# Moving a weight load to another DMA queue, moving two loads down a hand-written order, interleaving a rounding chain and closing a joint: an attention and MLP-mixer kernel

## The chip, the cores and the metric

The kernel runs on one core of one Trainium2 chip, as one launch. The metric is the device time in microseconds. The kernel before was run three times beside its profile: 807.25 us is the median, 807.18 the lowest and 807.42 the highest.

## The reference

There are 8 batches, 8 heads, 576 tokens and 64 elements to a head. First comes linear attention with a root-mean-square norm for each head; its output is laid out as 576 tokens by 512 features. On this a mixer works: a token mixing with a residual, then a channel mixing with a residual.

```python
kv  = einsum('bhsd,bhse->bhde', k, v)
out = einsum('bhsd,bhde->bhse', q, kv)
x   = out / sqrt(mean(out*out, -1) + 1e-6) * g_norm   # then (B, S, 512)
xt  = x.transpose(0, 2, 1)
u   = x + (maximum(xt @ w_tok1, 0) @ w_tok2).transpose(0, 2, 1)
y   = u + maximum(u @ w_ch1, 0) @ w_ch2
```

`w_tok1` is 576x256, `w_tok2` 256x576, `w_ch1` 512x1536 and `w_ch2` 1536x512. The weights reach the kernel as 64-bit floats, and the kernel makes 32-bit floats of them itself.

## The kernel before, in words

**Two halves.** Until about 200 us the kernel does attention and token mixing, two batches (a pair) at a time, four pairs. From there it does the channel mixing, in nine groups of 512 token rows; between the halves `u` lies in DRAM (`u_dram`).

**First half.** The order of the work is written out by hand, as strings of step names that `play` calls one after the other: `start`, `middle`, twice `steady`, and `last`. Each string runs the attention of one pair beside the token mixing of the pair before it. A name is one step: `kv10` multiplies k by v for half 0 of batch 1 of the pair, `e10` copies the product out of PSUM, `a2` multiplies q by it for a piece of tokens, `g`, `q`, `t` are the gain, the square and the sum over 64 elements of a piece, `m`, `r`, `i` make the inverse norm of a group of pieces, `s` and `p` scale with it on ScalarE and on GpSimd. `h` is the first token product (`hr` its rest, with the ReLU), `z` seeds a PSUM bank with the residual and `u` is the second token product, with its store to `u_dram`. The order in a string is the order on every engine and on every DMA queue; semaphores make one engine wait for another.

**Loads.** `l00` to `l11` load k and v of half a batch for the next pair. There are four buffers `k_in` and four `v_in`, so that `l00` can start once `kv00` of the present pair has been read. A load is four DMAs, 1.18 MB together. `lq0` and `lq1` load q. All of these, and the stores, are issued by SP's queue, in the order of the strings (`dma`, L114); only the very first v goes by ScalarE's queue.

**Weights.** A weight is fetched as raw 32-bit words (`raw`, four buffers, tag `raw`) and turned in eight steps, `block` (L202) and `decode` (L149): `fetch`, then `scale` on ScalarE (L163), then on VectorE `clamp` (L166), `shift` (L170), `sign` (L174), `power` (L183), `lower` (L187) and `both` (L118). The last step that reads `raw` is `lower`. Each step but the first two works on the result of the one before it; `part` has one buffer. The token weights are five blocks (`w00` to `w47` in the strings), the channel weights fourteen: eight of `w_ch1` (768 elements to a partition, one DMA of 786 KB) and six of `w_ch2` (1024 elements, two DMAs of 524 KB). The first four fetches of the channel weights are named in the strings, `f0` to `f3`; everything else of them is a stream (`stream`, L1048) of which a number in a string takes that many steps. In the stream `scale` of the next block goes beside `lower`, and the fetch of the block four further beside `both`.

**Second half.** The channel mixing multiplies with seven products in place of eight, twice nested. The first group does it once only (`channel1_once`, `channel2_once`), the other eight groups do both levels. A product is some matmuls into a PSUM bank; the sums are VectorE's. `channel2_once` has seven steps, `first, sixth, second, seventh, fifth, fourth, third`, with four PSUM banks from pool `m` (6 banks). `weave` (L1039) spreads VectorE work between the steps. After it all groups are one list of numbered places (`put`, `products`, `beside`); at a place first the product runs and then what was put beside it. In `outer` (L763) the first product of a group goes to a bank `a`, `read_first` copies it to a bank `ps_c` from pool `c` (2 banks), and later products are added into both.

**The joint** between the first group and the nested ones is this (L1217 to L1224): the next `xg` is fetched, and two matmuls of 128x384, whose result nobody reads, go into the two banks of pool `c`, one ahead of place 0 and one behind its product.

Of the kernel before, what the change touches and what calls it, by code (L numbers as in the profile page):

```python
# [19 lines left out]
def kernel(  # L20
# [32 lines left out]
    nc = tc.nc  # L53
# [60 lines left out]
    def dma(o, i, engine=nc.sync):  # L114
        keep(engine.dma_start(o, i))  # L115
# [83 lines left out]

        return flat if len(dst.shape) == 2 else flat.rearrange("p (a n) -> p a n", a=dst.shape[1])  # L200

    def block(n, loads, dst):  # L202

        raw = []

        def fetch():
            raw.append(stage.tile([P, n, 2], U32, name="raw", tag="raw", bufs=4))
            for o, i in loads(raw[0]):
                dma(o, i)

        def turn():
            t = raw[0]
            return t if len(dst.shape) == 2 else t.rearrange("p (a n) w -> p a n w", a=dst.shape[1])

        return (fetch,) + decode(dst, turn)
# [14 lines left out]
    def get_ch1(c, f):  # L230

        return block(2 * FQ, lambda raw: [(raw, words(moe_w_ch1)[ts(c, P), ts(f, 2 * FQ)])],
                     w_ch1[:, 2 * f + c // 2, c % 2:4:2])

    def get_ch2(f):

        a = 2 * (2 * f // NS)

        def loads(raw):
            t = raw.rearrange("p (h f n) w -> p f h n w", h=2, f=2)  # L240
            rows = words(moe_w_ch2)[ts(f, 2 * P)].rearrange("(f p) (h n) w -> f p h n w", f=2, h=2)
            return [(t[:, i], rows[i]) for i in range(2)]

        dst = w_ch2[:, a:a + 2, ds(2 * f % NS, 2)]
        return block(2 * DM, loads, dst.rearrange("p h f n -> p h (f n)"))

# [370 lines left out]
    def m_psum(shape, name):  # L619
        return late["m"].tile(shape, F32, name=name, tag="m")  # L620
# [82 lines left out]
    def channel2_once(g):  # L703

        shape = [P, 2, DH]
        x = xg[g]
        quarter = lambda i, j: x[:, 2 * i:2 * i + 2, ts(j, DH)]

        def product(n, ps, start, stop):
            for p in range(2):  # L710
                for s in range(NS):
                    matmul(ps[:, p], lhsT=late["once"][n - 1][:, s, p], rhs=w2_of(n)[:, s],
                           start=(start and p == 0 and s == 0), stop=stop,
                           skip_group_check=True)

        p1, p6, p7, p5 = (m_psum(shape, f"ps_w{n}") for n in (1, 6, 7, 5))
        t1, u2, u3 = (r_tile() for _ in range(3))

        def first():
            product(1, p1, True, False)  # L720
            copy(t1, p1)

        def sixth():
            product(6, p6, True, True)
            tensor_add(u2, p6, t1)

        def seventh():
            product(7, p7, True, False)
            tensor_add(u3, p7, u2)
            tensor_add(quarter(0, 1), quarter(0, 1), u2)  # L730
            tensor_add(quarter(1, 0), quarter(1, 0), u2)

        def fifth():
            product(5, p5, True, False)
            tensor_add(u3, p5, u3)
            tensor_add(quarter(1, 1), quarter(1, 1), u3)

        def second():
            product(2, p1, False, True)
            tensor_add(quarter(0, 0), p1, quarter(0, 0))  # L740

        def fourth():
            product(4, p7, False, True)
            tensor_add(quarter(1, 0), p7, quarter(1, 0))
            store(g, xg, 1)

        def third():
            product(3, p5, False, True)
            tensor_add(quarter(0, 1), p5, quarter(0, 1))
            store(g, xg, 0)  # L750

        return [first, sixth, second, seventh, fifth, fourth, third]
# [10 lines left out]
    def outer(place, size, mul, to, base=None, act=copy, onto=False):  # L763

        banks, t = {}, {}

        def product(n, name, start, stop):
            if start:
                banks[name] = m_psum([P, size], f"ps_{name}")
            mul(n, banks[name], start, stop)

        def temp(n, bufs):
            t[n] = late["tmp"].tile([P, FQ], F32, name=n, tag=n, bufs=bufs)[:, :size]
            t[n] = fit(t[n])
            return t[n]

        def fit(flat):
            return flat if size == P else flat.rearrange("p (w t) -> p w t", w=W)

        def read(o, i, j):

            if base:
                tensor_add(o, fit(banks["a"]), base(i, j))
            else:
                copy(o, fit(banks["a"]))

        def read_first():
            banks["c"] = late["c"].tile([P, DM], F32, name="ps_c")[:, :size]
            read(fit(banks["c"]), 0, 0)

        def write(i, j, name, n):
            tensor_add(to(i, j), fit(banks[name]), to(i, j) if onto else t[n])

        def put_on(i, j, n):
            if onto:
                tensor_add(to(i, j), to(i, j), t[n])  # L800

        def take(i, j, name, act):
            if onto:
                tensor_add(to(i, j), banks[name], to(i, j))
            else:
                act(to(i, j), fit(banks[name]))

        def at(n, name, start, stop, *steps):
            def all_of():
                product(n, name, start, stop)  # L810
                for step in steps:
                    step()

            products[place + PLACE[n]] = all_of

        at(1, "a", True, False, read_first)
        at(6, "a", False, False, lambda: read(temp("u2", 2), 0, 1))
        at(5, "b", True, False)
        at(7, "a", False, False, lambda: read(temp("u3", 1), 1, 1))
        at(2, "c", False, True, lambda: take(0, 0, "c", act))  # L820
        put(place + PLACE[7] + (1 if onto else 2), do(put_on, 1, 1, "u3"), do(write, 1, 1, "b", "u3"))
        at(4, "a", False, True, lambda: take(1, 0, "a", copy) if onto else read(to(1, 0), 1, 0))
        put(place + PLACE[4], do(put_on, 0, 1, "u2"))
        at(3, "b", False, True)
        put(place + PLACE[3] + 1, do(write, 0, 1, "b", "u2"))
# [219 lines left out]
                fill[done]()  # L1045
                done += 1

    def stream(blocks, ahead=4):  # L1048


        steps = [blocks[0][1]]
        for n, block in enumerate(blocks):
            steps += block[2:]
            for at, m, k in ((-2, n + 1, 1), (-1, n + ahead, 0)):
                if m < len(blocks):
                    steps[at] = do(lambda *fs: [f() for f in fs], steps[at], blocks[m][k])
        return iter(steps)

    def play(lines, after={}, **stages):

# [37 lines left out]
    for block in tok1[2:] + tok2:  # L1098
# [11 lines left out]
        "h010 t21 m2 r2", "a30 g30 q30 i2 p20", "a31 g31 q31 t30", "h011 t31 m3 r3 p21", "a40 i3 p30 g40 q40 p31",  # L1110
        "h012 h013 t40 m4 r4 w21 i4 s40 lq0 l10 l11"]
    middle = [
        "kv00 e00 w31 w22 w23 w24", "h10 w25 w26 w27 f1 -lq1 l00 w32 w33 w34", "kv01 e01 l01 w41 w35 w36 w37",
        "h11 f2 w42 w43 w44", "hr w45 w46 w47 f3", "a0 q00 g01 q01 g00 t00 t01", "u0 z2 1", "u1 1",
        "a1 q10 g11 q11 g10 t10 t11 m0 r0", "u2 i0 1", "kv10 e10 z4 s00", "u3 1 s01", "kv11 e11 1",
        "u4 1 z6", "a2 q20 g21 q21 g20 s10", "u5 t20 t21 2", "a4 q40 g41 q41 g40 lq0 l10 l11", "u6 t40 t41 2",
        "a3 q30 g31 q31 g30 lq1 s11", "u7 t30 t31 m2 r2 1 i2 p20 p21 s30", "u8 1 s31"]

    def steady(n0, n1):
        return [  # L1120
            "kv00 l00 e00 1 -s40", "h00 3", "kv01 l01 e01 1", "h01 3", f"a0 q00 g01 q01 g00 {n0}",
            "h10 1 t00 t01 2", "h11 4", "hr 2 z2", "a1 q10 g11 q11 g10 1", "kv10 l10 e10 t10 t11 m0 r0 1",
            "u0 i0 1", "kv11 l11 e11", "u1 1 s00", "u2 z4 1", "a2 q20 g21 q21 g20", "u3 s01 t20 t21",
            "u4 z6 1", "a4 q40 g41 q41 g40 lq0", "u5 s10 t40 t41 1", "a3 q30 g31 q31 g30 lq1",
            "u6 s11 t30 t31 m2 r2 1 i2 p20 p21 s30", f"u7 1 s31 {n1}", "u8 2"]

    attentions = [attention(0, ((0,), (1,), (2,), (3,), (4,)))]
# [3 lines left out]
    mixings.append(token_mixing(B // 2 - 1, range(2, 9), (0, 1)))  # L1131
    more = {f"w{n}{k}": f for n, b in enumerate(tok1 + tok2) for k, f in enumerate(b)}
    more |= {f"f{n}": b[0] for n, b in enumerate(channel)}
    rounding = stream(channel)

    def keep_warm(n):

# [75 lines left out]
             lambda: [f() for f in outer_u(1)], lambda: [f() for f in inner_u(1, 0, 7)]]  # L1213
    extra += [lambda: None] * (len(channel2_once_steps := channel2_once(0)) - len(extra))
    body = [step for pair in zip(channel2_once_steps, extra) for step in pair]
    weave(body, lasts + [f for fs, _ in inner2 for f in fs] + [f for _, f in inner1])
    fetch_x(1, 0)  # L1217
    fetch_x(1, 1)


    for place in range(2):
        t = late["c"].tile([P, DM], F32, name="ps_c")
        step = do(matmul, t[:, :FQ], lhsT=w_ch1[:, 0, 0, :P], rhs=w_ch1[:, 0, 0], start=True, stop=True)
        put(place, step) if place else step()  # L1224
    for n, (_, f) in enumerate(inner2):
        put(8 + n, f)
    for g in range(1, NG):
# [42 lines left out]
```

## Time and profile before

| what | value |
|---|---|
| median of three runs | 807.25 us |
| the profiled execution | 807.63 us, of which the span from first to last instruction is 805.8 us |
| busy in the span | TensorE 788.6 us (98%), VectorE 683.3 (85%), ScalarE 302.2 (38%), GpSimd 79.6 (10%) |
| granted TensorE clock | 0.999 |
| DMA | 175.51 MB, 218 GB/s over the span; 276 GB/s from 0 to 205 us |
| GpSimd | 75 instructions, none of them a DMA |

How to read it: TensorE has matmuls in flight nearly all the time, so the span can only get shorter where TensorE idles or does work that isn't needed. Where it idles is read from the timeline of TensorE, in which a bracket gives the idle time and what ended it. "SPq" is SP's queue, that is the time in which it issues a DMA; "PEld" is TensorE's load of weights. The DMA row of the page gives, for each fortieth of the span, how busy the 16 DMA engines were.

### The profile page before, as it was taken

The page shows a single profiled execution, that of the slowest core. Times are in us where ns is not written, and L with a number is a line of the kernel's source. Part 1 is how long each engine was busy: PE and PEld are TensorE (multiplying, and loading weights), DVE is VectorE, ACT ScalarE, POOL GpSimd, SP SyncE. Part 2 cuts the span into 40 slices and gives each one's busy share as a digit, 9 for nine tenths or more (in the row PEclk, how much of TensorE's full clock was granted, in tenths as well). Part 3 has the DMA queues.
Part 4 walks back from the last instruction along what each step waited for, and adds up shares of the span by engine and source line. Part 5 has one row for each costly group of instructions (what it writes and reads, how often), then busy time and mean ns, then how long its engine had stood idle before and what let it go on. Part 6 is the DMA issues. An engine that isn't in the chain of part 4 may idle for free.

```text
span 805.8 us, 17651 instructions
## 1 busy us (share of the span) xinstructions
PE 788.6 (98%) x7012; PEld 694.4 (86%) x7012; DVE 683.3 (85%) x1308; ACT 302.2 (38%) x838; POOL 79.6 (10%) x75
## 2 busy tenths in 40 slices
PE   6999999999999999999999999999999999999997
PEld 6645554544888899999999999999999999999997
DVE  4688989999886978978987997997898899799687
ACT  1357585664110134234234234332424423423331
POOL 1210101010000011012003003001101200300300
PEclk9999999999999999999999999999999999999999
DMA  9999998436458567468467648738836855863642
GB/s 289 320 345 351 334 354 304 158 119 208 150 175 294 194 210 239 131 221 267 149 201 240 201 153 259 234 118 262 265 119 217 262 166 181 250 201 123 218 147 83
DMA packets 97346, 175.51 MB, mean 218 GB/s; under 512 B 7024, under 2 KB 54128, under 8 KB 97264
## 3 DMA queue, kind: packets, MB, share of 16 engines
q1 hardware_dynamic: 95584, 172.65, 66.6%
q10 hardware_dynamic: 1680, 1.74, 0.7%
q8 instruction: 55, 0.90, 0.5%
q14 instruction: 27, 0.22, 0.1%
HBM read 137.79 MB, written 36.57 MB: 216 GB/s over the span
## 4 chain that ended last, share of the span: by engine, by line
PE 83%; DVE 6%; DMA 5%; ACT 3%; SPq 1%; issue 1%; ACTq 0%; DVEq 0%
PE ps_a L127 37%; PE ps_b L127 19%; PE ps_c L127 9%; PE ps_v L127 5%; PE ps_w L127 4%; PE ps_u L127 4%; DMA v_in<-in_v_dram 3%; PE ps_h L127 2%; ACT x L475 1%; SPq L115 1%; DMA raw<-in_moe_w_ch_dram 1%; DMA k_in<-in_k_dram 1%; DVE ms L442 1%; DVE part L187 1%; DVE x L421 1%; PE ps_o L127 1%
## 5 line engine op out<-in xcount | busy, mean ns | idle before, releaser
L124 ACT COPY u<-ps_a 128x128 f32<-128x128 f32 (+1 forms) x160 | 56.1, 351 | 156.6 <-PE ps_a L127 156.6
L118 POOL TENSOR_TENSOR v<-v,v 128x384 f32<-128x384 f32 (+1 forms) x48 | 61.4, 1301 | 532.8 <-ACT v L124 492.8
L127 PE MATMUL ps_b<-uT,sums 128*128 128x128 f32 x672 | 86.2, 276 | 0.0
L127 PEld LDWEIGHTS ps_b<-uT,sums 128*128 128x128 f32 x672 | 80.7, 192 | 0.2
L118 DVE TENSOR_TENSOR v<-v,v 128x768 f32<-128x768 f32 (+1 forms) x86 | 79.5, 932 | 1.1
L127 PE MATMUL ps_a<-uT,w_ch 128*128 128x128 f32 x576 | 78.9, 275 | 0.0
L124 ACT COPY ps_c<-ps_a 128x128 f32<-128x128 f32 (+1 forms) x80 | 26.9, 336 | 129.5 <-PE ps_a L127 129.5
L118 DVE TENSOR_TENSOR v<-ps_b,u 128x384 f32<-128x384 f32 x112 | 61.5, 549 | 12.3 <-PE ps_b L127 10.6
L127 PEld LDWEIGHTS ps_a<-uT,w_ch 128*128 128x128 f32 x576 | 71.4, 192 | 0.4
L127 PE MATMUL ps_u<-h,w_tok 128*128 128x512 f32 (+1 forms) x160 | 68.0, 608 | 1.6 <-ACT h L121 0.6
L127 PE MATMUL ps_h<-x,w_tok 128*128 128x512 f32 (+1 forms) x160 | 65.9, 604 | 0.0
L118 DVE TENSOR_TENSOR uT<-uT 128x512 f32<-128x512 f32 (+4 forms) x103 | 63.1, 629 | 0.8
L127 PE MATMUL ps_a<-uT,w 128*128 128x128 f32 x432 | 60.0, 275 | 0.0
L127 PEld LDWEIGHTS ps_a<-uT,w 128*128 128x128 f32 x432 | 54.0, 192 | 0.0
L127 PEld LDWEIGHTS ps_h<-x,w_tok 128*128 128x128 f32 (+1 forms) x160 | 25.9, 189 | 31.1 <-issue 28.3
L127 PEld LDWEIGHTS ps_u<-h,w_tok 128*128 128x128 f32 (+1 forms) x160 | 24.5, 178 | 31.9 <-issue 24.9
L121 ACT ACTIVATE v<-v 128x384 f32<-128x384 f32 (+1 forms) x86 | 42.5, 528 | 23.0 <-DVE v L118 22.5
L118 DVE TENSOR_TENSOR sv<-v 128x384 f32<-128x384 f32 x80 | 43.4, 551 | 8.9 <-ACT v L121 8.9
L118 DVE TENSOR_TENSOR xg<-xg,r 128x512 f32<-128x512 f32 x74 | 50.0, 686 | 0.7
L475 ACT ACTIVATE x<-x,inv 128x64 f32<-128x64 f32 x184 | 46.0, 336 | 9.6 <-DVE inv L461 9.6
L127 PE MATMUL ps_a<-sums,sv 128*128 128x128 f32 x336 | 47.1, 276 | 0.0
L127 PE MATMUL ps_a<-uT,sums 128*128 128x128 f32 x336 | 46.8, 275 | 0.0
(134 smaller groups left out, 1576.5 us busy)
## 6 DMA issues: line engine op xcount, KB each, us to landing
sums<-sums SPq DMA_DIRECT2D x112, 576.0 KB, 4.4
qT<-in_q_dram SPq DMA_DIRECT2D x8, 1152.0 KB, 9.6
xt<-u_dram SPq DMA_DIRECT2D x36, 256.0 KB, 4.0
blocks<-y SPq DMA_DIRECT2D x72, 128.0 KB, 2.7
uT<-blocks SPq DMA_DIRECT2D x36, 256.0 KB, 4.9
xg<-u_dram SPq DMA_DIRECT2D x18, 512.0 KB, 5.1
k_in<-in_k_dram SPq DMA_DIRECT2D x16, 512.0 KB, 9.2
u_dram<-x SPq DMA_DIRECT2D x16, 512.0 KB, 4.9
```

Of the source, the lines that this page charges most:

```text
L115: keep(engine.dma_start(o, i))
L118: keep(engine.tensor_tensor(out=o, in0=a, in1=b, op=op))
L121: keep(nc.scalar.activation(o, a, AF.Relu))
L124: keep(nc.scalar.copy(o, a))
L127: keep(nc.tensor.matmul(*a, **kw))
L187: keep(nc.vector.scalar_tensor_tensor(out=part[0], in0=raw()[..., 0], scalar=2.0 ** -52, in1=part[0], op0=ALU.mult, op1=ALU.mult))
L421: keep(nc.vector.tensor_mul(x, bank[c, h], g_sb.to_broadcast([P, number(c), D])))
L442: keep(nc.vector.tensor_reduce(stats_of(c)[0][:, h], sq[c, h], axis=AX.X, op=ALU.add))
L475: keep(nc.scalar.activation(x[:, k, h], x[:, k, h], AF.Copy, scale=inv[:, k, h]))
```

## The change

It has four parts.

- **Loads later.** `l00` to `l11` of `middle` and `steady` stand further down in the strings. One number of `middle` (`u8 1`) is now 2.
- **Rounding in turns.** For the six blocks of `w_ch2` the stream no longer does the six VectorE steps of a block in a row: `clamp`, `shift`, `sign` of a block alternate with `power`, `lower`, `both` of the block before. `scale` of the next block goes beside `shift`, and the fetch of the block four further beside `lower`. Blocks of `w_ch1` stay as they were.
- **Joint.** The two matmuls without a reader are gone. `channel2_once` takes two of its four banks (`p7`, `p5`) from pool `c`; its last step, `third`, runs behind the first product of place 0, and the two fetches of `xg` behind that.
- **Queue.** The fetches of the channel weights are issued by GpSimd's queue, those of the token weights by SP's as before. GpSimd keeps its scalings `p` in its own order with them.

```diff
-    def block(n, loads, dst):
+    def block(n, loads, dst, engine=nc.sync):
...
-                dma(o, i)
+                dma(o, i, engine)
...
-                     w_ch1[:, 2 * f + c // 2, c % 2:4:2])
+                     w_ch1[:, 2 * f + c // 2, c % 2:4:2], nc.gpsimd)
...
-        return block(2 * DM, loads, dst.rearrange("p h f n -> p h (f n)"))
+        return block(2 * DM, loads, dst.rearrange("p h f n -> p h (f n)"), nc.gpsimd)
...
-        p1, p6, p7, p5 = (m_psum(shape, f"ps_w{n}") for n in (1, 6, 7, 5))
+        p1, p6 = (m_psum(shape, f"ps_w{n}") for n in (1, 6))
+        p7, p5 = (late["c"].tile(shape, F32, name="ps_c", tag="c") for _ in range(2))
...
-            banks["c"] = late["c"].tile([P, DM], F32, name="ps_c")[:, :size]
+            banks["c"] = late["c"].tile([P, DM], F32, name="ps_c", tag="c")[:, :size]
...
-    def stream(blocks, ahead=4):
+    def stream(blocks, turns, ahead=4):
+        def all_of(*fs):
+            return do(lambda: [f() for f in fs])
         steps = [blocks[0][1]]
-        for n, block in enumerate(blocks):
-            steps += block[2:]
-            for at, m, k in ((-2, n + 1, 1), (-1, n + ahead, 0)):
-                if m < len(blocks):
-                    steps[at] = do(lambda *fs: [f() for f in fs], steps[at], blocks[m][k])
-        return iter(steps)
+        second = []
+        for n in range(len(blocks)):
+            _, _, *first = blocks[n]
+            if n + 1 < len(blocks):
+                k = 1 if n >= turns else 4
+                first[k] = all_of(first[k], blocks[n + 1][1])
+            if n + ahead < len(blocks):
+                k = 4 if n >= turns else 5
+                first[k] = all_of(first[k], blocks[n + ahead][0])
+            if n < turns:
+                steps += first
+            else:
+                pairs = zip(first[:3], second or [None] * 3)
+                steps += [f for pair in pairs for f in pair if f]
+                second = first[3:]
+        return iter(steps + second)
...
     middle = [
-        "kv00 e00 w31 w22 w23 w24", "h10 w25 w26 w27 f1 -lq1 l00 w32 w33 w34", "kv01 e01 l01 w41 w35 w36 w37",
-        "h11 f2 w42 w43 w44", "hr w45 w46 w47 f3", "a0 q00 g01 q01 g00 t00 t01", "u0 z2 1", "u1 1",
+        "kv00 e00 w31 w22 w23 w24", "h10 w25 w26 w27 f1 -lq1 w32 w33 w34", "kv01 e01 w41 w35 w36 w37",
+        "h11 f2 w42 w43 w44", "hr l00 w45 w46 w47 f3", "a0 q00 g01 q01 g00 t00 t01", "u0 z2 1", "u1 l01 1",
...
-        "u4 1 z6", "a2 q20 g21 q21 g20 s10", "u5 t20 t21 2", "a4 q40 g41 q41 g40 lq0 l10 l11", "u6 t40 t41 2",
-        "a3 q30 g31 q31 g30 lq1 s11", "u7 t30 t31 m2 r2 1 i2 p20 p21 s30", "u8 1 s31"]
+        "u4 1 z6", "a2 q20 g21 q21 g20 s10", "u5 t20 t21 2", "a4 q40 g41 q41 g40 lq0", "u6 t40 t41 2 l10",
+        "a3 q30 g31 q31 g30 lq1 s11", "u7 t30 t31 m2 r2 1 i2 p20 p21 s30", "u8 2 l11 s31"]
     def steady(n0, n1):
-            "kv00 l00 e00 1 -s40", "h00 3", "kv01 l01 e01 1", "h01 3", f"a0 q00 g01 q01 g00 {n0}",
-            "h10 1 t00 t01 2", "h11 4", "hr 2 z2", "a1 q10 g11 q11 g10 1", "kv10 l10 e10 t10 t11 m0 r0 1",
-            "u0 i0 1", "kv11 l11 e11", "u1 1 s00", "u2 z4 1", "a2 q20 g21 q21 g20", "u3 s01 t20 t21",
-            "u4 z6 1", "a4 q40 g41 q41 g40 lq0", "u5 s10 t40 t41 1", "a3 q30 g31 q31 g30 lq1",
+            "kv00 e00 1 -s40", "h00 3", "kv01 e01 1", "h01 3", f"a0 q00 g01 q01 g00 l00 {n0}",
+            "h10 1 t00 t01 2", "h11 l01 4", "hr 2 z2", "a1 q10 g11 q11 g10 1", "kv10 e10 t10 t11 m0 r0 1",
+            "u0 i0 1", "kv11 e11", "u1 1 s00 l10", "u2 z4 1", "a2 q20 g21 q21 g20", "u3 s01 t20 t21",
+            "u4 z6 1 l11", "a4 q40 g41 q41 g40 lq0", "u5 s10 t40 t41 1", "a3 q30 g31 q31 g30 lq1",
...
-    rounding = stream(channel)
+    rounding = stream(channel, 2 * NC)
...
     body = [step for pair in zip(channel2_once_steps, extra) for step in pair]
+    behind = body.pop(-2)
     weave(body, lasts + [f for fs, _ in inner2 for f in fs] + [f for _, f in inner1])
-    fetch_x(1, 0)
-    fetch_x(1, 1)
-    for place in range(2):
-        t = late["c"].tile([P, DM], F32, name="ps_c")
-        step = do(matmul, t[:, :FQ], lhsT=w_ch1[:, 0, 0, :P], rhs=w_ch1[:, 0, 0], start=True, stop=True)
-        put(place, step) if place else step()
+    put(0, behind, do(fetch_x, 1, 0), do(fetch_x, 1, 1))
```

## The prediction

> **What bounds the kernel now.** I read the page first, then TensorE's timeline for its gaps, then the chain of waits.
>
> ```profile
> PE   6999999999999999999999999999999999999997
> DVE  4688989999886978978987997997898899799687
> DMA  9999998436458567468467648738836855863642
> ```
>
> TensorE is full after the first fortieth. DMA is full for six to seven slices (to about 135 us), and VectorE is nearly full from slice 5 to 10. The span is 805.8 us and TensorE busy 788.6, so 17.2 us are idle: 6.7 ahead of the first matmul, about 5 in the tail (21.1 us busy from 780 to 806), the rest, some 5.5, in small gaps between 20 and 165 us. From 165 to 780 us there is none: a microsecond saved before it is a microsecond of the result.
>
> The gaps that the change can reach, from the timelines of TensorE, ScalarE and VectorE:
>
> ```profile
> 26.13 1.39 PE L127 MATMUL ps_kv<-v_in,k_in 128*64 128x64 f32 x40 [0.94 <-DMA v_in<-in_v_dram]
> ...
> 100.00 0.94 ACT L163 ACTIVATE w_ch<-raw 128x768 f32<-128x768 f32 x1 [7.70 <-DMA raw<-in_moe_w_ch_dram]
> ...
> 103.93 0.69 DVE L421 TENSOR_TENSOR x<-ps_o,g_sb 128x512 f32<-128x512 f32 x1 [1.68 <-ACT sq L425]
> ...
> 161.93 1.16 PE L127 MATMUL ps_o<-kvp,qT 64*64 64x64 f32 x64 [1.12 <-ACT sq L425]
> ```
>
> Read the bracket: the idle time, and what ended it. `kv11` of the first pair waits for its v. At 100 us ScalarE has stood 7.7 us before a `scale` whose raw weight is late; behind it stand the ReLUs of `hr` and the squares, so VectorE loses 1.68 us and TensorE 0.57. At 161.93 `a3` waits for a square, which waits for a gain (L421) that stands behind rounding in VectorE's queue.
>
> The chain of waits (start, length, what) says how the first and the second came about:
>
> ```profile
> 15.82 10.17 DMA v_in<-in_v_dram
> 26.13 1.39 PE ps_kv L127 x40
> ...
> 79.20 9.54 DMA v_in<-in_v_dram
> 88.75 2.00 SPq L115
> 90.85 9.13 DMA raw<-in_moe_w_ch_dram
> 100.95 1.95 ACT h L121 x4
> ```
>
> A load of v lands, only then does SP's queue come to the raw fetch.
>
> **The Trainium skill.** (1) "DMA: Bandwidth & Descriptors", section "Issuing engines are not separate DMA queues": DMAs of all issuers run on the same 16 engines and interleave, and "Queues, rings and completion order": an engine goes round-robin between its queue rows. The trace agrees as far as it goes: from 15 to 27 us the engines are over-full (share 1.09) at 331 GB/s. So another queue is no more bandwidth, but it gets its turn beside SP's. (2) The same page, "SWDGE vs HWDGE vs iDMA": GpSimd makes descriptors in software, into SBUF; first byte after about 1 us against 0.6. No run shows it here; the kernel before has no such DMA. (3) "SBUF — State Buffer", "Who interferes with whom": GpSimd and VectorE share a port pair, and the later one blocks. The trace agrees for GpSimd's arithmetic: beside the GpSimd scaling of 124.20, a `power` takes 1.25 us where 0.56 is usual, a `lower` 1.70 where 0.96 is. (4) "VectorE: DVE Perf Modes", "The DRAIN you can't avoid", says that a semaphore between VectorE operations costs nothing extra. The trace differs for neighbours that depend: `lower` to `both` of 768 elements is 1.00 us start to start, an independent neighbour starts after 0.88.
>
> **The change, part by part.**
>
> *Joint.*
>
> ```profile
> 272.79 0.81 PE L127 MATMUL ps_c<-w_ch 128*128 128x384 f32 x2
> 273.44 0.83 PE L127 MATMUL ps_a<-uT,w_ch 128*128 128x128 f32 x6
> 274.11 0.81 PE L127 MATMUL ps_c<-w_ch 128*128 128x384 f32 x2
> 274.82 0.94 PE L127 MATMUL ps_a<-uT,sums 128*128 128x128 f32 x6
> ```
>
> The two unread matmuls hold TensorE from 272.79 to 273.44 and from 274.11 to 274.82: 1.36 us go. In their place `third` (5.2 us) covers the copy of bank `a`. New: `read_first` now needs a bank of pool `c`, which VectorE must first have read for `fourth`. Adding up VectorE's new order from 257.45 on with the old durations, this read ends at 273.4, the copy (0.46) at 273.95, while `third` ends at 273.45: 0.5 us of wait, less the 0.1 that the old fourth line lost. VectorE's last read of `p5`, at 277.4, comes just in time for the next copy. Gain 1.0 us; ends 0 (VectorE 1 us later) and 1.4. `xg` is fetched some 2 us later and first used 18 places on: nothing.
>
> *Queue, later fetches.* In the built program the fetch of block 5 waits only for `lower` of block 1 (at 83.2) and two GpSimd scalings (to 84.1), not for the loads ahead of it in SP's queue: 84.1 in place of 90.85. With 1 us for software and half the bandwidth (0.786 MB at 165 GB/s is 4.8 us) it lands about 92, when ScalarE gets there (92.3). So the 7.7 us go. TensorE gets 0.57 there and most of 0.6 in the following small gaps (0.28 at 112.1, 0.3 at 116.7): 1.0 us; ends 0.4 and 1.3.
>
> *Queue, first fetches.* This is the cost. In SP's order `f0` was behind the loads and was issued late:
>
> ```profile
> 16.05 0.69 DVE L187 SCALAR_TENSOR_TENSOR part<-raw,part 128x512 f32<-128x512 uint32 x1
> ...
> 35.77 0.34 SPq L115 DMA_DIRECT2D raw<-in_moe_w_ch_dram  x1
> ```
>
> Its buffer is free when that `lower` (the second token block) ends, at 16.74. GpSimd has nothing ahead of it, so `f0` goes out at about 17, in the midst of the 10.17 us in which the v of `kv11` comes. Its 786 KB share the engines with that load and are through before it: 786 KB at 331 GB/s are 2.4 us, at the 390 GB/s of the best windows 2.0. `kv11` has no slack (it waits already), nor has the chain behind it. I take 2.1 us lost; ends 0 (if SP's descriptors keep precedence) and 2.4. The bytes are missing later, from 36 on, where nobody waits for them: nothing gained. `f1` to `f3` come 2 to 11 us sooner, beside `l10` and `l11` of the first `middle`; these land about 57, by 62 then, and are used at 60.5 and 63.7 plus the 2.1: covered.
>
> *Queue, port.* Twenty descriptor makings of about 1 us each. `f1` and `f2` fall at 46 to 51 us beside the rounding of `w_tok2`, on which TensorE waits at 54.75; later ones follow a `lower`, beside `both` (two inputs) and the next `clamp`. Bounds: 0, and 1 us for each of the first two plus a third of the ten up to 160 us, 5 us of VectorE, of which the gaps let some 3.5 reach TensorE. I take 0.7. GpSimd's scalings behind a fetch are delayed by 1 us; `h00` and `h01` of the next string read them, after `kv` and four tiles: covered.
>
> *Loads later.* The place in a string matters only relative to SP's other DMAs. `l00` of `middle` still follows `lq1` at once (about 50). `l01` now waits for `u1`'s store (60), `l11` for `u8`'s (84), `l10` of `steady` for `u1`'s (109). With 10 us to landing they are there at 71, 95, 119, and needed at 84, 104, 144. The last load of q lands near 130 and is needed at 133. Nothing lost; what is won is counted with the fetches.
>
> *Turns.* Neighbours that depend on each other among the `w_ch2` steps: 18 before, 4 after, at 0.12 us: 1.7 us of VectorE. Seven lie before 162 us, 0.85, and 0.55 us less rounding stands ahead of `a2`'s gain. Of the 1.12 and 0.26 us of gaps in the second `steady` 0.6 go; ends 0 and 1.4. In `last` TensorE doesn't wait for VectorE: nothing. The number 2 only moves a step from `last` to `middle`.
>
> *Sum.* 2.1 + 0.7 - 1.0 - 1.0 - 0.6 = +0.2 us on the profiled 807.63, or about 807.4 on the median, which is 0.38 lower. Since the gains' ends lie further out than I took them, I say 807.2: no change.
>
> **The rivals.**
> - *No toll at the start* (0.29): SP's loads are not held up by `f0`, or `kv11` makes it good. For it: the skill gives no share, and GpSimd's first fetch could come late. Against: the engines are over-full. Then 807.25 - 2.6 + 0.7 - 0.4 (gains at their better half) = 805.0.
> - *The shared port decides* (0.33): descriptor making blocks VectorE, which is 95% busy from 80 to 200 us. For it: the rows at 124.20. Against: most rounding steps could block it instead. From about 2 us of VectorE on the path (0.2 us a fetch in the ten, or the first two fully) the gains are used up; at 3.3 us in place of 0.7 it is 807.2 + 2.6 = 809.8.
> - *The loads don't move*: SP was so far behind that `l10`, `l11` went late anyway (101.8 to 111.9 before). That is so for half of them; if the early fetch too brought nothing, 807.2 + 0.8 = 808.0, within the forecast's case.
>
> **Numbers.** Forecast, no measurable change, 0.38: 805.7 to 808.8 (0.2%, 1.6 us, is about what a measurement of this kernel can tell). Faster 0.29, at 803.5 to 805.6. Slower 0.33, 808.9 to 811. The range 804.4 to 810.3 leaves a tenth out at each side.
>
> **What would show it.** Right: `kv11` of the first pair at about 28.2 with an idle bracket of some 3 us; no wait of `scale` for raw at 100; the first `ps_v` later by 0.5 to 1.5 us than 200.2; from `third` on about 1 us regained; `clamp` or `shift` of 0.6 to 1.5 us beside fetches. Wrong: `kv11` at 26.1, or VectorE's busy time up by over 5 us, or a new wait of `kv` for v or k after 60 us.

## The result, and the profile after

| kernel | executions | median, us | lowest to highest |
|---|---|---|---|
| before | 4 | 807.34 | 807.18 to 807.55 |
| changed | 4 | 807.53 | 807.34 to 808.98 |
| before, run again beside e9 to e11 | 46 | 807.41 | 806.33 to 809.24 |
| changed, run again (e11) | 10 | 808.98 | 807.14 to 810.97 |

The first set gives a ratio of 1.0006 (0.9989 to 1.0023), no difference. The second, with more executions, gives 1.0019 (1.0008 to 1.0030): slower by some 1.5 us, just at what a measurement can tell. The changed kernel has two kinds of executions, as will be seen; the profiled one (808.98 us, span 807.2) is of the slower kind.

The page of the changed kernel: first the busy time (engine, us, share, instructions), then the rows in fortieths.

```profile
PE 788.1 (98%) x7008; PEld 694.4 (86%) x7008; DVE 682.2 (85%) x1308; ACT 301.4 (37%) x838; POOL 92.8 (11%) x95
...
PE   6899999999999999999999999999999999999997
...
DVE  4588999999786978978987997997898899799687
```

VectorE's busy time did not rise (683.3 before). GpSimd has 20 instructions and 13 us more. TensorE's second slice, 20 to 40 us, fell from 9 to 8, which is small on the page and turns out to be what matters most. The gaps of before, in the timelines of TensorE, ScalarE and GpSimd (start, length, what, idle time ahead and what ended it):

```profile
27.44 1.42 PE L127 MATMUL ps_kv<-v_in,k_in 128*64 128x64 f32 x40 [2.10 <-DMA v_in<-in_v_dram]
...
157.83 1.98 PE L127 MATMUL ps_u<-h,w_tok 128*128 128x512 f32 x4 [0.56 <-ACT ps_u L124]
...
163.82 1.16 PE L127 MATMUL ps_o<-kvp,qT 64*64 64x64 f32 x64 [1.12 <-ACT sq L425]
```

```profile
94.54 1.72 ACT L163 ACTIVATE w_ch<-raw 128x768 f32<-128x768 f32 x2
100.94 0.60 ACT L121 ACTIVATE h<-ps_h 128x512 f32<-128x512 f32 x1 [4.67 <-PE ps_h L127]
```

```profile
17.14 0.71 POOL L115 DMA_DIRECT2D raw<-in_moe_w_ch_dram  x1 [13.72 <-DVE part L187]
```

At the start `kv11` waits 2.10 us in place of 0.94, with `f0` issued at 17.14, as forecast (with some 3 us of wait). The 7.70 us for which ScalarE stood at 100 us are gone: it scales early and now waits for TensorE's product. But the gap ahead of `a3` is still 1.12, and the one on `ps_u` has grown from 0.26 to 0.56. In the chain of waits the same load of v (from 15.8 or 15.9 us on) has become 1.2 us longer than the 10.17 of before:

```profile
15.95 11.36 DMA v_in<-in_v_dram
```

The second pair's first `kv00` is 2.77 us late (42.95 against 40.18), though `kv11` is only 1.31 late (27.44 against 26.13). The windows of TensorE say where the rest arose. Columns: window, its length, busy TensorE (instructions), granted clock, DMA share, GB/s.

```profile
26.00:28.00 2.00, 0.56 (x19) 1.00 1.05 365
28.00:30.00 2.00, 2.00 (x34) 0.67 1.09 312
30.00:32.00 2.00, 2.00 (x4) 0.50 1.05 298
32.00:34.00 2.00, 2.00 (x6) 0.98 0.98 367
```

Soon after the idle 2.10 us the granted clock is 0.50 for 3.41 us (28.7 to 32.1 in the trace's clock record). From `kv00` at 42.95 on, the kernel regains time: 1.14 us by the second `steady` string (125.01 against 123.38), and 0.8 at the joint, of which this is the timeline:

```profile
269.50 0.83 PE L127 MATMUL ps_a<-uT,w_ch 128*128 128x128 f32 x6
270.17 5.35 PE L127 MATMUL ps_c<-w_ch,v 128*128 128x256 f32 x24
275.74 0.94 PE L127 MATMUL ps_a<-uT,sums 128*128 128x128 f32 x6 [0.22 <-ACT ps_c L124]
```

The matmuls without a reader are gone, `third` stands behind the first product, and 0.22 us of wait for the copy is left.

### The profile page after: what moved, and what is told of

The parts are those of the page before. It is cut to its first block, busy times and chain, and to the rows that moved or that the text cites. A ratio compares the mean times of both kernels' runs of the same rounds, so it can differ in the third digit from the quotient of the medians.

```text
span 807.2 us, 17655 instructions
## 1 busy us (share of the span) xinstructions
PE 788.1 (98%) x7008; PEld 694.4 (86%) x7008; DVE 682.2 (85%) x1308; ACT 301.4 (37%) x838; POOL 92.8 (11%) x95
## 4 chain that ended last, share of the span: by engine, by line
PE 78%; DVE 12%; DMA 4%; ACT 3%; issue 1%; SPq 0%; DVEq 0%; ACTq 0%
PE ps_a L127 37%; PE ps_b L127 19%; PE ps_c L127 10%; PE ps_v L127 5%; PE ps_u L127 3%; PE ps_h L127 3%; DMA v_in<-in_v_dram 2%; PE ps_w L127 2%; DMA k_in<-in_k_dram 2%; DVE ms L442 2%; DVE x L421 2%; ACT x L475 2%; DVE part L187 1%; DVE w_ch L174 1%; DVE w_ch L118 1%
## 5 line engine op out<-in xcount | busy, mean ns | idle before, releaser
L127 PEld LDWEIGHTS ps_u<-h,w_tok 128*128 128x128 f32 (+1 forms) x160 | 24.5, 179 | 31.2 <-issue 24.9
```

The costliest lines, as they stand in the source:

```text
L127: keep(nc.tensor.matmul(*a, **kw))
```

## The experiments

The theory: four terms add up. A toll at the start by `f0`, doubled by the clock; a gain of about 1 us from the fetches; about 0.8 from the joint; nothing from turns and port. The rivals: the turns are worth their 0.6 us, the port costs VectorE something, or `kv11` is late for another reason.

A time scatters by some 1.5 us either way: the kernel before has 805.88 to 809.24 us over the 128 executions beside e1 to e11. In the traces such differences are short waits, for a DMA or for VectorE, that come and go. The stages before 280 us repeat better from trace to trace: where `f0` doesn't go out early, the start lies between 39.87 and 40.57 us. So each run is given twice, as the median with its ratio to the kernel before, and as stage lengths from the starts of TensorE's `ps_kv` groups and of the first `ps_v`, the first product of the second half: the first `kv00` of the second pair ("start"), from the first `kv00` of the one `steady` string to that of the other ("steady 1"; 79.01 to 123.38 us before), from there to the first `ps_v` ("rest"; 200.17 us before), and, for the joint, by how much the distance changed between two ScalarE copies, those at 211.56 and 287.40 us of the kernel before. The `middle` string, between start and steady 1, takes 38.8 us in every trace.

| kernel | start | steady 1 | rest | joint | median, us | median of before beside it | ratio (95%) |
|---|---|---|---|---|---|---|---|
| before | 40.18 | 44.37 | 76.79 | 0 | | | |
| changed (e11 for the time) | 42.95 | 43.23 | 77.05 | -0.81 | 808.98 | 807.41 | 1.0019 (1.0008 to 1.0030) |
| e1 joint alone | 39.87 | 43.84 | 76.77 | -0.81 | 806.76 | 807.49 | 0.9992 (0.9984 to 1.0000) |
| e2 queue alone | 43.19 | 42.93 | 77.01 | 0 | 809.79 | 807.49 | 1.0024 (1.0013 to 1.0034) |
| e3 changed, `f0` late | 39.96 | 43.24 | 77.06 | -0.80 | 806.37 | 807.49 | 0.9988 (0.9981 to 0.9994) |
| e4 changed, old turns | 44.67 | 43.25 | 77.40 | -0.81 | 809.92 | 807.49 | 1.0033 (1.0020 to 1.0046) |
| e5 changed, gap filled | 41.29 | 43.24 | 77.05 | -0.81 | 807.98 | 807.52 | 1.0006 (0.9998 to 1.0014) |
| e6 joint, queue, `f0` late | 40.32 | 42.93 | 76.97 | -0.81 | 806.27 | 807.52 | 0.9984 (0.9977 to 0.9991) |
| e7 loads alone | 40.16 | 42.95 | 77.27 | -0.01 | 806.66 | 807.52 | 0.9992 (0.9984 to 1.0000) |
| e8 turns alone | 40.27 | 44.35 | 76.84 | 0 | 807.52 | 807.52 | 0.9999 (0.9991 to 1.0007) |
| e9 joint and loads | 39.93 | 42.93 | 77.28 | -0.82 | 805.84 | 807.41 | 0.9982 (0.9975 to 0.9988) |
| e10 changed, `f0` on SP | 40.57 | 43.21 | 77.07 | -0.82 | 806.03 | 807.41 | 0.9984 (0.9977 to 0.9990) |

One term is in no column. From the start of VectorE's last instruction to the end of the span, the five kernels without a fetch on GpSimd's queue take 4.12 to 4.31 us, and the nine with one 4.37 to 4.61 us (4.14 before, 4.61 changed). So with this queue the end takes some 0.2 to 0.5 us more. What happens there the profile doesn't show.

**e1, the joint alone.**

```diff
-        p1, p6, p7, p5 = (m_psum(shape, f"ps_w{n}") for n in (1, 6, 7, 5))
+        p1, p6 = (m_psum(shape, f"ps_w{n}") for n in (1, 6))
+        p7, p5 = (late["c"].tile(shape, F32, name="ps_c", tag="c") for _ in range(2))
...
+    behind = body.pop(-2)
...
+    put(0, behind, do(fetch_x, 1, 0), do(fetch_x, 1, 1))
```

> The kernel before with the joint edit alone. Joint theory (the two PSUM buffers and the missing pair of spacer matmuls let the first product of block 1 start about 1.0 us sooner): 1.0 us below the kernel before, the product prod7 at 275.3 us where the kernel before had 276.33, everything ahead of 259 us unmoved. Rival (the gap only moves to the first wait of the next block): within 0.3 us of the kernel before.

`prod7`, the product that starts at 276.33 us in the kernel before, came at 274.50 us. Of these 1.83 us, 0.85 had been there at the first `ps_v`, so 0.98 is the joint's at that product; 0.81 of it is left at 287 us, the same within 0.01 us in the eight traces of the table that have the new joint. The median fell by 0.73, with an interval that just reaches 1. In this execution TensorE's wait of 0.57 us at 102 us happened not to be, though ScalarE stood 7.17 us there: with the old order of loads and fetches steady 1 is 43.84 us or some 44.4, as it comes.

**e2, the queue alone.**

```diff
-                     w_ch1[:, 2 * f + c // 2, c % 2:4:2])
+                     w_ch1[:, 2 * f + c // 2, c % 2:4:2], nc.gpsimd)
...
-        return block(2 * DM, loads, dst.rearrange("p h f n -> p h (f n)"))
+        return block(2 * DM, loads, dst.rearrange("p h f n -> p h (f n)"), nc.gpsimd)
```

> The kernel before with the fetches of the channel weights on GpSimd's queue and nothing else. Toll theory (the first fetch, now 30 us earlier on its own queue, takes a share of the bandwidth from the last of v, and the wait of ScalarE at 100 us is gone): kv11 at 27.4 instead of 26.13 us (+1.3), about 0.6 us regained at 100 us, so +0.7 us at the end (+2.2 where the clock falls to half after the longer idle). Rival (the shared port: descriptors made by GpSimd hold VectorE up, 16 fetches): +2 us or more at the end, with clamp and shift above 0.8 us beside most fetches.

From TensorE's timeline and windows:

```profile
27.75 2.08 PE L127 MATMUL ps_kv<-v_in,k_in 128*64 128x64 f32 x40 [2.59 <-DMA v_in<-in_v_dram]
```

```profile
28.00:30.00 2.00, 2.00 (x40) 0.54 1.10 350
30.00:32.00 2.00, 2.00 (x6) 0.60 1.05 338
```

The loss is there: the start is 3.0 us later, steady 1 is 1.4 shorter, the rest is 0.2 longer and the end 0.5. That makes 2.3, as the profiled executions have it (809.88 against 807.63). In steady 1 too the port costs nothing that shows: 42.93 us, as in e9, which has no fetch on GpSimd. The toll is what makes this kernel 2.3 us slower in the median; the port is not.

**e3, the first fetch late.** The changed kernel with

```diff
-        "kv00 e00 l00 j14 w01 w11 w02 w03 w04 w05 w06 w07 w12 w13 w14 w15 w16 w17", "kv01 j10 e01 l01 f0",
+        "kv00 e00 l00 j14 w01 w11 w02 w03 w04 w05 w06 w07 w12 w13 w14 w15 w16 w17", "kv01 j10 e01 l01",
...
-        "kv10 j6 t11 m1 r1 e10 i1 s10 p11", "kv11 j2 e11", "h000 h001 h002 h003", "a20 g20 q20", "a21 g21 q21 t20",
+        "kv10 j6 t11 m1 r1 e10 i1 s10 p11", "kv11 j2 e11", "h000 h001 h002 h003 f0", "a20 g20 q20", "a21 g21 q21 t20",
```

> The changed kernel with its first fetch (f0) issued after the first four h products, not after kv01. Toll theory (f0 beside the last v load is what delays kv11): kv11 back at 26.1 us, the shift of +1.3 (or +2.8 with the clock at half) at 40 us gone, and the time 1.3 us (2.8 in an execution with the dip) below the changed kernel: about 806.2 us. Rival (kv11 is late by something else in the start, and f0 only lies beside it): kv11 stays at 27.4 and the time at 807.5 us.

```profile
26.09 1.39 PE L127 MATMUL ps_kv<-v_in,k_in 128*64 128x64 f32 x40 [0.94 <-DMA v_in<-in_v_dram]
```

`kv11` is back to the tenth, the clock stays at 1.00, and the median is 806.37. `f0` goes out at 28.49 here, behind that load. So it is `f0` beside the load of v that makes the start late; with this one word moved, the change is a gain of 1.1 us.

**e4, the turns undone.** The changed kernel with

```diff
-    rounding = stream(channel, 2 * NC)
+    rounding = stream(channel, len(channel))
```

> The changed kernel with the rounding of the second channel weight one block after the other, as before; the rest as changed. My prediction's term (turns save a dependent step's delay on VectorE): 0 to 0.6 us above the changed kernel. Rival, after the trace of the changed kernel (the last attention stage and the h products after it gained nothing, +0.26): within 0.3 us of the changed kernel or below it.

Neither fits by the time (809.92), because the start differs: here `kv11` waited 2.83 us and the clock stayed at half for 6.83 us, two such stretches. By stages the turns are worth 0.35 us in company of the other parts (rest 77.40 without, 77.05 with), on this wait of the second `steady` string:

```profile
160.48 1.98 PE L127 MATMUL ps_u<-h,w_tok 128*128 128x512 f32 x4 [1.48 <-ACT ps_u L124]
...
165.73 1.35 PE L127 MATMUL ps_o<-kvp,qT 64*64 64x64 f32 x64 [0.73 <-ACT sq L425]
```

It is 0.56 and 1.12 with them (157.83 and 163.82 above). In the kernel before, 1.48 was 0.26: this is a wait that the change itself lets grow, and that the turns partly take back.

**e5, the gap filled.** The changed kernel with

```diff
-        "kv10 j6 t11 m1 r1 e10 i1 s10 p11", "kv11 j2 e11", "h000 h001 h002 h003", "a20 g20 q20", "a21 g21 q21 t20",
+        "kv10 j14 t11 m1 r1 e10 i1 s10 p11", "kv11 j2 e11", "h000 h001 h002 h003", "a20 g20 q20", "a21 g21 q21 t20",
```

> The changed kernel with 8 more of the dummy matmuls on ident (ps_j, 275 ns each, 2.2 us) behind kv10, where TensorE sat idle for 2.1 us ahead of kv11. Clock theory (the longer idle lets the granted clock fall to 0.50 for one stretch of 3.41 us, which costs 1.5 us beside the 1.3 of the wait itself): no stretch at 0.50, kv11 still at about 27.4, kv00 of the second pair at about 41.5 us and not 42.95, and the time about 807.2 us with no execution above 808.5. Rival (the clock falls there for another reason): the stretch at 0.50 stays, some executions at 809 and more.

```profile
26.00:28.00 2.00, 2.00 (x34) 1.00 1.10 389
28.00:30.00 2.00, 2.00 (x34) 1.00 1.07 279
30.00:32.00 2.00, 2.00 (x6) 1.00 1.01 312
```

`kv11` starts at 27.41 as before the filling, no stretch is at half, and `kv00` comes at 41.29: 1.66 us for the clock, 1.11 for the late v. The other executions agree: one stretch at half takes 0.002 off the mean clock, so with one it is 0.998 at most, and 12 of the 13 have 0.999 or 1.000. As to the clock this settles it. The median is 807.98, though, 0.8 above what I expected, and three of 13 executions lie above 808.5. At least the profiled execution (809.22) shows where it lost: short waits in the second half, 0.38 us at 288 for `sums` and two on VectorE at 368 and 566, which cost it about 2 us together:

```profile
288.45 0.91 PE L127 MATMUL ps_a<-uT,sums 128*128 128x128 f32 x6 [0.38 <-DMA sums<-sums]
...
368.38 0.94 PE L127 MATMUL ps_a<-uT,w_ch 128*128 128x128 f32 x6 [0.47 <-DVE u L118]
```

Such waits come and go here. Whether the longer median is more than them, this run does not tell.

**e6, joint and queue, with `f0` late; loads and turns as before.** The edits are those of e1, e2 and e3 on the kernel before.

> The kernel before with the joint edit and GpSimd's queue, the first fetch late as in e3; loads and turns as before. If loads and turns are worth nothing: within 0.3 us of e3 (806.4 us), first ps_v at about 199.1 us. Rival (the later loads are what takes the wait of ScalarE at 100 us away, or the turns are worth their 0.6): 0.5 to 1.5 us above e3, with the wait of 0.57 us on h at 102 us back.

806.27 us against 806.37 for e3, first `ps_v` at 199.04: beside the queue, the later loads and the turns bring nothing (by the stages they even cost 0.4 us: 43.24 and 77.06 in e3, 42.93 and 76.97 here).

**e7, the later loads alone.**

```diff
-            "kv00 l00 e00 1 -s40", "h00 3", "kv01 l01 e01 1", "h01 3", f"a0 q00 g01 q01 g00 {n0}",
-            "h10 1 t00 t01 2", "h11 4", "hr 2 z2", "a1 q10 g11 q11 g10 1", "kv10 l10 e10 t10 t11 m0 r0 1",
+            "kv00 e00 1 -s40", "h00 3", "kv01 e01 1", "h01 3", f"a0 q00 g01 q01 g00 l00 {n0}",
+            "h10 1 t00 t01 2", "h11 l01 4", "hr 2 z2", "a1 q10 g11 q11 g10 1", "kv10 e10 t10 t11 m0 r0 1",
...
```

(and so on, in `middle` too, as in the change)

> The kernel before with the later loads of k and v alone, all fetches on SP's queue. If GpSimd's queue alone removed the wait at 100 us: within 0.3 us of the kernel before. Rival (on one queue the later loads let the raw fetches pass ahead, which is enough): about 1.0 us below it, the wait of 0.57 us on h at 102 us gone. A third way: a later load is late for its kv product, a new wait of TensorE on k_in or v_in after 60 us, slower by its length.

SP's queue issues the raw fetches sooner, at 83.16 and 88.77, where the kernel before came to its fetch only at 90.85:

```profile
83.16 0.64 SPq L115 DMA_DIRECT2D raw<-in_moe_w_ch_dram  x1
83.85 1.13 SPq L115 DMA_DIRECT2D k_in<-in_k_dram  x2
85.03 3.64 SPq L115 DMA_DIRECT2D v_in<-in_v_dram  x2
88.77 0.52 SPq L115 DMA_DIRECT2D raw<-in_moe_w_ch_dram  x1
```

and steady 1 is 42.95, as short as with the queue. The rival was right: either part alone removes the wait of ScalarE. The median fell by 0.86, again with an interval that just reaches 1. Of the 1.42 us gained in steady 1, 0.48 go again in the rest, where the wait on `ps_u` is now 1.34 us (it was 0.26):

```profile
155.54 1.98 PE L127 MATMUL ps_u<-h,w_tok 128*128 128x512 f32 x4 [1.34 <-ACT ps_u L124]
```

No `kv` waits for its load after 60 us.

**e8, the turns alone.**

```diff
-    rounding = stream(channel)
+    rounding = stream(channel, 2 * NC)
```

> The kernel before with the rounding in turns alone. My prediction's term: 0 to 0.6 us below the kernel before. Rival (VectorE isn't what the stage waits for): within 0.2 us of it, with the second steady stage at 45.1 us, as before.

Nothing: ratio 0.9999, every stage within 0.1 us of the kernel before, the wait ahead of `a3` still 1.1.

**e9, joint and loads, all on SP's queue.** The edits of e1 and e7 together.

> The kernel before with the joint edit and the later loads, all fetches on SP's queue, rounding as before. Sum of the two parts run alone (joint -1.0 in its trace, loads -1.0 in its trace): first ps_v at 199.2 us, prod7 at about 274.4 us, the time 1.5 to 2.0 us below the kernel before. Rival (the two gains overlap, or the random waits of the tail cover them): as with the joint alone, 0.7 us below.

805.84 us, 1.57 below, with `prod7` at 274.13. The medians of e1 and e7 (0.73 and 0.86) add up to 1.59.

**e10, `f0` on SP's queue.** The changed kernel with

```diff
-                     w_ch1[:, 2 * f + c // 2, c % 2:4:2], nc.gpsimd)
+                     w_ch1[:, 2 * f + c // 2, c % 2:4:2], nc.gpsimd if c + f else nc.sync)
```

> The changed kernel with its first fetch (f0) alone on SP's queue, in its place in the text; the other fetches on GpSimd's. If the toll comes of f0 having a line of its own (it starts at 17 us beside the loads of v that SP's line has ahead of it): kv11 back at 25.5 to 26.1 us, no stretch at 0.50 of the clock, kv00 at 40.2 us, the time as in e3, about 806.3 us. Rival (f0 delays v from any queue): kv11 at 27.4 us and the time at 807.5 us or above.

`kv11` starts at 25.52 without a gap and the median is 806.03: the four parts with their first fetch left in SP's line gain 1.38 us. SP comes to `f0` at 35.11, so this run, like e3, moves its time; it doesn't part the queue from the time. With e6 and e9 it is the best version here; the three can't be told apart, and all beat both kernels, by 0.2% of the one before.

**e11, the changed kernel again.**

> The changed kernel once more, for the spread of its executions. Clock theory: two kinds of executions, one with the stretch at half the clock and one without it, some 1.5 us apart, so more width than the kernel before has; the median 0 to 1 us above it. Rival (the stretch was that one execution's): the executions spread as those of the kernel before, with a median 0.5 us below them.

Three of the ten executions took 807.14 to 807.44 us, seven 808.68 to 810.97. Six of these seven have a mean clock of 0.997 or less, the other four executions 0.998 and more; one stretch of 3.41 us at half takes 0.002 off the mean over 806 us. (In the tail, where TensorE is done, the clock falls too and takes up to 0.002 as well, so 0.998 alone decides nothing.) The theory holds, with more executions of the slower kind than the first set showed (one of four). The seventh is the profiled one (808.68): it had an idle time of 2.25 us ahead of `kv11` and no stretch; its start is 1.4 us late (41.62), and two waits for `sums` in the second half cost it 0.7.

Why did 2.25 us leave the clock at 1.00 here, where 2.10 did not? The clock records answer it. In all fourteen traces the first stretch at full clock is a whole number of pieces of 3.413 us (17.07 us is five, 791.89 is 232), so the pieces can be laid over TensorE's time. In the changed kernel the 2.10 us lie in one piece, from 25.26 to 28.68, and the clock falls at its end. Here a border of pieces, at 27.26, cuts the idle time in two:

```profile
23.84:27.26 3.42, 1.66 (x17) 1.00 1.06 339
27.26:30.67 3.41, 2.92 (x47) 1.00 1.07 313
```

That is 1.76 and 0.49 us idle. Over all pieces of all traces, the tails included, the clock fell from 1.00 behind each one with 2.00 us or more of idle TensorE and behind none with 1.85 or less. The pieces lie anywhere against the kernel (the first border in the records is between 9.2 and 12.9 us of the span), so the same gap costs the stretch in some executions and not in others.

**e12, `f0` on ScalarE's queue.** As e10, with `nc.scalar` in place of `nc.sync`.

> The changed kernel with its first fetch (f0) alone on ScalarE's queue, in its place in the text (behind the first two scalings of w_tok, so free to start at about 14 to 17 us); the other fetches on GpSimd's. Bandwidth theory (0.79 MB moved between 15 and 27 us from any line but SP's takes 2.3 us of the 344 GB/s from the loads of v): kv11 at 27.4 us again, idle ahead of it over 2 us, the time as the changed kernel's, 808 to 809 us, in two kinds. Rival (it is GpSimd's queue, slow or served ahead of the others, that delays v): kv11 at 25.5 to 26.1 us and about 806.1 us, as in e10.

813.0 us against 807.70 (1.0061, 1.0047 to 1.0076), and no answer. The fetch went out only at 24.9 us, and ScalarE, which works in order, stood before it until, as the trace reads it, a load of k landed, with the squares behind. The waits and TensorE's timeline:

```profile
ACT sq L425 <- DMA k_in<-in_k_dram: 12.1, 1, 12.1
```

```profile
25.99 3.78 PE L127 MATMUL ps_o<-kvp,qT 128*128 128x128 f32 x16 [5.96 <-ACT sq L425]
```

Whether `f0` beside SP's line costs bandwidth only, or whether GpSimd's queue is served ahead, stays open. What it adds is one more point on the clock: 5.96 us idle, two stretches (6.83 us) at half.

## Why the prediction was right, and where it was not

"No measurable change" is what the first set shows and what the sum gave. The second set, at 1.5 us slower, has its median at 808.98, 0.2 us past the end of that forecast (805.7 to 808.8). That only one of the first four executions had the stretch at half clock, and six of the later ten, was luck. Step by step:

- *First fetches, +2.1 (0 to 2.4).* The mechanism was right in each step: `f0` out at 17 us, the same load of v longer (11.36 for 10.17 us), `kv11` late, undone by e3 and by e10. The term was mis-sized, because it lacked the clock. The load alone costs 1.1 to 1.4 us (start 41.29 in e5, 41.62 in e11, against 40.18, give or take 0.4 by the scatter of the start), less than the bytes of `f0` over the bandwidth had given. With one stretch at half clock it is 2.8 to 3.0 (42.95, 43.19), with two 4.5 (e4): above my upper end. So the first `ps_v` came 1.9 us late in the profiled execution (202.06), where I had forecast 0.5 to 1.5. I had read the idle time as the whole cost of an idle TensorE. The Trainium skill, "TensorE: Matmul & The Clock Gate", section "What's actually happening", has the rule: full rate falls to half after a window of 3413 ns in which TensorE is idle, and the windows run free of the kernel. The length agrees exactly (3.41 and 6.83 us), and so does the free running (the pieces of e11 and of the changed kernel lie differently). The condition does not: 2.00 us of idle time in a window were enough. That is why gaps of 2.10, 2.59 and 2.83 us brought the half clock, and the 2.25 us of e11, cut in two, did not.
- *Queue, later fetches, -1.0 (-0.4 to -1.3).* Right in size: -1.14 in steady 1 (-0.6 against the trace of e1, where TensorE's wait happened not to be). But I put it to the queue, and the loads do the same alone (e7). Together they bring no more than one: 43.23, against 42.93 for either. What makes up those 0.3 us was not isolated.
- *Loads later, 0.* Wrong alone (-0.86), right as an addition to the queue (e6 beside e3). My rival "the loads don't move" asked only if they go late anyway; I hadn't asked which fetches of SP's queue then pass ahead of them.
- *Joint, -1.0.* 0.98 at `prod7`, 0.81 some ten us on, 0.73 in the medians. The remaining wait is 0.22 us where I had worked out 0.5.
- *Port, +0.7 (0 to 3.5).* 0.2 us at most, the lengthening of the rest in e2. An issue takes GpSimd 0.53 to 0.83 us, less than the 1 us that I had taken from the Trainium skill, "DMA: Bandwidth & Descriptors" (a first-byte latency, given in its section "Specifications"). Only few VectorE steps beside an issue are longer. This is the fetch of 103.40, the two DMAs of one block, with the two steps beside it, 0.73 and 0.69 us where 0.55 is usual:

```profile
103.40 1.44 POOL L115 DMA_DIRECT2D raw<-in_moe_w_ch_dram  x2 [5.32 <-ACT h L121]
```

```profile
103.75 0.73 DVE L166 TENSOR_SCALAR w_ch<-w_ch 128x768 f32<-128x768 f32 x1
104.51 0.69 DVE L170 TENSOR_SCALAR w_ch<-w_ch 128x768 uint32<-128x768 uint32 x1
```

- *End.* A term that the prediction didn't have: the 0.2 to 0.5 us by which a kernel with GpSimd's queue takes longer at its end.
- *Turns, -0.6.* Failed: 0.0 alone, and -0.35 only on a wait that the other parts had let grow. The step that failed is the one from 0.55 us less rounding ahead of `a2`'s gain to 0.6 us less of the gaps: VectorE may have saved its time, but the square and the copy of `ps_u` that TensorE waits for came no sooner. I had counted VectorE's work and not followed the ordering from the gain to the wait.

So the sum came out at about zero for partly wrong reasons: the toll without the clock was too large by about 0.8 us, the port by 0.5, the turns by 0.3 to 0.6 the other way, and the end was missing. In stages, the profiled execution has +2.77 - 1.14 + 0.26 - 0.81 + 0.47 (end) = +1.55 us, and ended 1.35 above that of the kernel before; with the starts of e5 and e11, which have no stretch, the sum is -0.1 to +0.2, and the executions of the changed kernel without one lie at 807.1 to 807.6, but for the 808.68 of e11.

Of the rivals, "no toll" is refuted as a case (e3 and e10 show that there is one), and its price, 805.0, is 1.0 us (e10) to 1.4 us (e3) below what comes out when `f0` is put elsewhere. "The shared port decides" named about the time of the slower executions, 809.8, but by a mechanism that costs 0.2 us at most.

## What to carry to other kernels

When a transfer gets a queue of its own, look first at what it can now overtake or run beside: here one fetch issued 18 us sooner cost one to two times what all the rest of the change gained, and with that one fetch left in the old line the same change is 1.4 us faster than the kernel before. Price an idle TensorE of 2 us and more not by its length alone but with the half clock that may follow. And test two cures of one wait singly: two parts that each remove it don't add, and the next wait (here the copy of `ps_u`) takes part of the gain.

## What the runs showed of the hardware

- The granted clock falls to 0.50 in whole stretches of 3.41 us after idle times of TensorE of 2.10 us (one stretch), 2.59 (one), 2.83 (two) and 5.96 (two); 0.94 us, 2.02 at 14.68 us of e5 and 2.25 in e11 left it at 1.00. Counted in pieces of 3.413 us from the first clock record, it fell from 1.00 behind every piece with 2.00 us or more of idle TensorE (2.00 and 2.06 in the tails of e10 and e9, 2.08 in e4, 2.11 in the changed kernel, 2.59 in e2, 3.41 in e12) and behind none with 1.85 (the tail of e6) or less, as far as the modelled ends of the matmuls go. At half clock, a piece with 0.74 us idle (e4) or 1.52 (e12) kept it there, and one without idle time ended it. With the gap filled by matmuls nobody reads, it stayed at 1.00 (e5).
- A DMA issued by GpSimd (128 partitions of 6 or 4 KB) occupies GpSimd 0.53 to 0.83 us; the eight of 6 KB land after 7.9 us in the median, the twelve of 4 KB after 6.6. These 20 lengthened neither VectorE's busy time (682.2 against 683.3) nor, beyond 0.2 us, the stages behind the start. The span ends 4.37 to 4.61 us after the start of VectorE's last instruction where GpSimd issues DMAs, and 4.12 to 4.31 where it doesn't.
- A single load under a full DMA (share 1.05 to 1.1) went from 10.17 to 11.36 us (11.65 in e2) when 786 KB on another queue were moved beside it, and was back at 10.12 when they were issued later on that queue (e3).
